# A retention layer with a low-rank mixer and MLP: paired batches, chunk-wise attention and an interleaved order of work

## Chip, cores, metric

One core of one Trainium2 chip. The metric is the device time of one execution in microseconds (us); lower is better. "Before" is the tuned kernel given, "after" the changed one. Matmuls write their results to PSUM; VectorE and ScalarE read them from there (an "evacuation").

## The reference

Batch 8, 8 heads, 576 tokens, head size 64, model width 512, MLP width 2048, mixer rank 32. Inputs and output are float32; both kernels calculate in bf16 with float32 accumulation.

```
scores = (q @ k.T) / sqrt(64);  ret = scores * gamma_h ** (i - j) for i >= j, else 0
x      = concat_heads(ret @ v)                      # 576 x 512 per batch
u      = x + (V.T @ U.T @ x)                        # mixer over tokens, rank 32
out    = u + relu(u @ w_ch1) @ w_ch2
```

Retention is computed in chunks of 128 tokens. gamma^i goes into q and gamma^-j into v. Within a chunk the scores are masked; across chunks a running state of k.T v is carried along. 576 = 4 x 128 + 64, so the last chunk is half full.

## The kernel before

Attention works on one pair of heads at a time, over all five chunks. `# ...` marks cuts.

```python
def attention_hp(hp, q_all, k_all, v_all, x_t):
    # ... transposes of q and k for 5 chunks, q scaled, k copied
    po = ps_out.tile([P, 8, P], FP32, tag="ps_out", name="po")
    for c in range(NC - 1):                       # running state, one matmul at a time
        nc.tensor.matmul(po[:, 5 + (c % 2), :], k2d, v2d, start=True, stop=True)
        # ... VectorE adds it to the state before, head by head (64 x 64)
    for c in range(NC - 1):                       # scores: 64 rows = one head
        for hl in range(2):
            pb = hl * 64
            nc.tensor.matmul(sc_h[hl][:, c, :], kT[pb:pb + 64, ...], qT[pb:pb + 64, ...], ...)
    # ... masks; then the scores of the last chunk, one matmul per head
    for c in range(NC):                           # ret @ v, 128 rows, 64 columns
        # ...
    for c in range(1, NC):                        # q @ state: 64 rows, 64 columns
        for hl in range(2):
            nc.tensor.matmul(po[:, slot, 0:64], qT[pb:pb + 64, ...], S_list[c - 1][pb:pb + 64, :], ...)
    # ... VectorE adds this to x

def mlp_tail(b, u_t, uT_t):
    for f in range(NF):                           # first layer: 2 x 288 columns
        for half in range(2):
            # 4 matmuls into ps_y1, then relu
    for tcn in range(NC):                         # second layer: 5 chunks, the last with 64 tokens
        for f in range(NF):
            nc.tensor.matmul(ps_y2[0:L, :], y1_t[:, f, tcn * P:tcn * P + L], w2_sb[:, f, :], ...)
        # ... add u, store
```

GpSimd issues all loads (they cast to bf16) and also scales v. A scheduler decides how attention of batch b+1 is mixed into the MLP of batch b.

## Time and profile before

| | before |
|---|---|
| median time | 432.16 us (13 runs, 431.71 to 432.77) |
| span of the profiled run | 430.0 us |
| first MLP matmul | 60.16 us |
| distance from batch to batch | 47.39 us |
| busy: TensorE / VectorE / ScalarE / GpSimd | 91 / 51 / 40 / 39 % |

TensorE is full from 60 us on. A full TensorE isn't yet one at its peak: its busy time is built from modelled ends, so what counts is the distance from one matmul's start to the next. The prediction shows the lines of this profile.

### The profile page before, as it was taken

To read this page: it belongs to the slowest core of one execution; us is meant where nothing else is said; L and a number is where in the kernel's file an instruction comes from. 1 tells how busy PE (TensorE), PEld (TensorE's weight loads), DVE (VectorE), ACT (ScalarE), POOL (GpSimd) and SP (SyncE) were. 2 spreads that over 40 slices of the span, in tenths; PEclk is the share of its full clock that TensorE was granted. 3 is DMA by queue.
4 is the path that set the end of the run, shared out by engine and by line. 5 is a ranking of instruction groups with operands and counts; after the bars stand their busy time and mean duration, and the time that the engine had idled before them with its cause. 6 is when DMAs were issued, how large, how long until landed. Compare 5 with 4: busy or idle time off the path is not lost.

```text
span 430.0 us, 8035 instructions
## 1 busy us (share of the span) xinstructions
PE 391.8 (91%) x3248; PEld 232.1 (54%) x3248; DVE 220.9 (51%) x662; ACT 171.9 (40%) x379; POOL 169.3 (39%) x220
## 2 busy tenths in 40 slices
PE   1256489999999999999999999999999999999996
PEld 0034256754675457644665467645765467546742
DVE  0166458751775448652875268643875277541011
ACT  2152136630564226630664136531663046423800
POOL 9999669999976700691048500000000000000000
PEclk9999999999999999999999999999999999999999
DMA  9999899999949910891079810011000100011011
GB/s 72 93 64 109 159 202 152 60 145 107 169 29 89 110 61 2 58 135 73 14 49 80 113 38 2 2 49 63 2 1 26 65 22 2 2 50 61 2 49 62
DMA packets 121333, 28.38 MB, mean 66 GB/s; under 512 B 114096, under 2 KB 116176, under 8 KB 121296
## 3 DMA queue, kind: packets, MB, share of 16 engines
q0 software_dynamic: 116048, 18.43, 57.8%
q1 hardware_dynamic: 5248, 9.44, 6.2%
q8 instruction: 25, 0.41, 0.4%
q14 instruction: 12, 0.10, 0.1%
HBM read 36.85 MB, written 9.44 MB: 108 GB/s over the span
## 4 chain that ended last, share of the span: by engine, by line
PE 87%; POOL 4%; DVE 4%; ACT 3%; issue 1%; DVEq 0%; ACTq 0%; POOLq 0%
PE ps_y L356 33%; PE ps_y L341 30%; PE po L185 3%; PE po L256 3%; PE ps_h L312 3%; PE blk_sc L219 3%; PE ps_at L301 2%; PE psq L164 2%; PE psk L174 2%; PE ps_ut L325 2%; PE po L271 2%; PE blk_sct L238 2%; ACT x_t L264 1%; POOL q_all L141 1%; POOL k_all L141 1%
## 5 line engine op out<-in xcount | busy, mean ns | idle before, releaser
L341 PE MATMUL ps_y<-uT_t,w_sb 128*128 128x288 bf16 x1024 | 155.3, 287 | 0.0
L356 PE MATMUL ps_y<-w_sb,y_t 128*128 128x512 bf16 (+1 forms) x640 | 149.6, 379 | 0.0
L347 ACT ACTIVATE y_t<-ps_y 128x288 bf16<-128x288 f32 x226 | 93.1, 412 | 62.7 <-PE ps_y L341 54.2
L341 PEld LDWEIGHTS <-w_sb 128*128 128x128 bf16 x1024 | 88.6, 98 | 27.8 <-issue 1.4
L356 PEld LDWEIGHTS <-y_t 128*128 128x128 bf16 (+1 forms) x640 | 61.5, 100 | 65.3 <-issue 3.4
L363 DVE TENSOR_TENSOR o_sb<-ps_y,u_t 128x512 f32<-128x512 f32 (+1 forms) x40 | 27.6, 690 | 99.5 <-PE ps_y L356 99.5
L177 ACT COPY kT<-psk 128x640 bf16<-128x640 bf16 x32 | 22.2, 693 | 95.7 <-PE psk L174 95.7
L200 DVE TENSOR_TENSOR S_cur<-po,S_cur 64x64 bf16<-64x64 f32 x192 | 42.3, 220 | 20.0 <-PE po L185 15.4
L227 DVE TENSOR_TENSOR ret_m<-blk_sc,maskbin 128x512 bf16<-128x512 f32 x64 | 42.5, 687 | 12.7 <-PE blk_sc L219 8.3
L150 POOL TENSOR_TENSOR v_all<-v_all,vscale 128x512 bf16<-128x512 bf16 x40 | 41.4, 1054 | 4.4 <-DMA v_all<-in_v_dram 3.9
L318 DVE TENSOR_TENSOR u_t<-ps_h,x_t 128x512 bf16<-128x512 f32 x40 | 27.6, 690 | 27.3 <-PE ps_h L312 27.3
L185 PE MATMUL po<-v_all,k_all 128*128 128x128 bf16 x128 | 29.2, 228 | 9.7 <-POOL v_all L150 4.7
L330 ACT COPY uT_t<-ps_ut 128x512 bf16<-128x512 bf16 x40 | 23.4, 586 | 33.8 <-PE ps_ut L325 33.8
L141 POOL DMA_DIRECT2D q_all<-in_q_dram x40 | 34.2, 875 | 0.0
L141 POOL DMA_DIRECT2D v_all<-in_v_dram x40 | 34.0, 912 | 0.0
L141 POOL DMA_DIRECT2D k_all<-in_k_dram x40 | 33.7, 874 | 0.0
L280 DVE TENSOR_TENSOR x_t<-po,x_t 128x192 bf16<-128x192 f32 x64 | 22.5, 351 | 7.8 <-PE po L271 5.5
L195 DVE CAST S_cur<-po 64x64 bf16<-64x64 f32 x64 | 14.1, 220 | 24.0 <-PE po L185 23.5
L264 ACT CAST x_t<-po 128x512 bf16<-128x512 f32 x31 | 18.2, 586 | 17.7 <-PE po L256 16.9
L164 PE MATMUL psq<-ident,q_all 128*128 128x128 bf16 x160 | 16.4, 230 | 8.8 <-DMA q_all<-in_q_dram 8.7
L138 POOL MEMSET q_all<- 64x512 bf16 x8 | 4.2, 520 | 50.2 <-PE psq L164 50.0
L185 PEld LDWEIGHTS <-k_all 128*128 128x128 bf16 x128 | 12.7, 100 | 18.4 <-issue 4.4
(50 smaller groups left out, 313.5 us busy)
## 6 DMA issues: line engine op xcount, KB each, us to landing
out_dram<-o_sb SPq DMA_DIRECT2D x32, 256.0 KB, 2.0
q_all<-in_q_dram POOLq DMA_DIRECT2D x32, 128.0 KB, 4.3
k_all<-in_k_dram POOLq DMA_DIRECT2D x32, 128.0 KB, 4.4
v_all<-in_v_dram POOLq DMA_DIRECT2D x32, 128.0 KB, 4.6
w_sb<-in_moe_w_ch_dram POOLq DMA_DIRECT2D x4, 512.0 KB, 7.5
w_sb<-in_moe_w_ch_dram POOLq DMA_DIRECT2D x16, 128.0 KB, 5.3
out_dram<-o_sb SPq DMA_DIRECT2D x8, 128.0 KB, 2.2
q_all<-in_q_dram POOLq DMA_DIRECT2D x8, 64.0 KB, 4.8
```

The lines of the kernel that those rows point to most:

```text
L141: nc.gpsimd.dma_start(out=t_sb[0:L, c, :, :], in_=t_dram[b, :, c * P:c * P + L, :].rearrange("h s d -> s h d"),)
L150: nc.gpsimd.tensor_tensor(out=v_all[:, c, :, :], in0=v_all[:, c, :, :], in1=vs_b[:, c, :, :], op=ALU.mult,)
L164: nc.tensor.transpose(psq[:, c, :], q2d, ident)
L185: nc.tensor.matmul(po[:, 5 + (c % 2), :], k2d, v2d, start=True, stop=True,)
L200: nc.vector.tensor_tensor(out=S_cur[pb:pb + 64, :], in0=po[pb:pb + 64, 5 + (c % 2), pb:pb + 64], in1=S_list[c - 1][pb:pb + 64, :], op=ALU.add,
L227: nc.vector.tensor_tensor(out=rt_h[hl][:, :, :], in0=sc_h[hl][:, :, :], in1=maskbin[:, None, :].to_broadcast([P, 4, P]), op=ALU.mult,)
L318: nc.vector.tensor_tensor(out=u_t[:, c, :], in0=ps_h, in1=x_t[:, c, :], op=ALU.add)
L330: nc.any.tensor_copy(out=uT_t[:, :, c * P:(c + 1) * P], in_=ps_ut[:, 0:NCC, :])
L341: nc.tensor.matmul(ps_y1[:, 0:HTOK], w1_sb[:, cc, f * P:(f + 1) * P], uT_t[:, cc, t0:t0 + HTOK], start=(cc == 0), stop=(cc == NCC - 1),)
L347: nc.any.tensor_scalar(out=y1_t[:, f, t0:t0 + HTOK], in0=ps_y1[:, 0:HTOK], scalar1=0.0, scalar2=None, op0=ALU.max,)
L356: nc.tensor.matmul(ps_y2[0:L, :], y1_t[:, f, tcn * P:tcn * P + L], w2_sb[:, f, :], start=(f == 0), stop=(f == NF - 1),)
L363: nc.vector.tensor_tensor(out=o_sb[0:L, :], in0=ps_y2[0:L, :], in1=u_t[0:L, tcn, :], op=ALU.add,)
```

## The change

Its intent is to do less on TensorE and to keep it fed evenly:

1. two batches share their half-full chunks, so that an even batch has 4 and an odd batch 5 full chunks in the MLP (mean 4.5 instead of 5);
2. attention goes chunk by chunk over all heads; the running state stays in PSUM and is read by one VectorE operation per chunk for all heads (masked to its diagonal blocks, which makes q @ state a matmul on all 128 rows); gamma^i is applied at the output;
3. loads go chunk by chunk (k, q, v), and v of the first two batches is scaled on VectorE;
4. an explicit order spreads attention and mixer items evenly through the MLP;
5. small PSUM pools have one buffer each; relu is on ScalarE only.

The diff, cut to its core (`...` marks cuts; most lines of the kernel changed):

```diff
+def interleave(main, fill):
+    ...
+        if j >= len(fill) or (i < len(main) and dm / tm <= df / tf):   # next MLP item
+        ...                                                              # else next attention item
-    def attention_hp(hp, q_all, k_all, v_all, x_t): ...
+    def load_chunk(b, c):
+        for j, dram in ((1, k), (0, q), (2, v)):
+            nc.gpsimd.dma_start(out=t[rows, j, :, :], in_=dram[b, :, t0:t0 + L, :]...)
+        (nc.vector if b < 2 else nc.gpsimd).tensor_tensor(out=t[rows, 2, :, :], ...)   # scale v
+        def ST(c):                                  # state of all heads, accumulated in PSUM
+            for hp in range(NHP):
+                nc.tensor.matmul(pss[:, hp, :], k..., v...,
+                    start=(c == 0 and hp == 0), stop=True, skip_group_check=True)
+            nc.vector.tensor_tensor(out=s_sb, in0=pss, in1=bdm..., op=ALU.mult)
+        def SC(c):                                  # eight score matmuls together
+            for hp in range(NHP):
+                for hl in range(2):
+                    pb = hl * HALF
+                    nc.tensor.matmul(psc[:, hl, hp, 0:n], qkT[pb:pb + HALF, NHP + hp, :],
+                                     qkT[pb:pb + HALF, hp, cols], start=True, stop=True)
+        def RV(c):                                  # ret @ v, then q @ state on 128 rows
+            ...
+                    nc.tensor.matmul(po[:, hp * P:(hp + 1) * P], qkT[:, hp, :], s_sb[:, hp, :],
+                                     start=False, stop=True, skip_group_check=True)
-        for f in range(NF):
-            for half in range(2): ...               # 128 matmuls of 288 columns a batch
+        nch = 4 if par == 0 else 5
+        segs = [(0, 512)] if par == 0 else [(0, 320), (320, 320)]
+    early_consts(); zero_halves(); load_batch(0); late_consts()
+    load_batch(1); load_w1(); load_w2()
+    interleave([], front_items(0))
+    for b in range(B): ...
+            interleave(mlp_items(b, us[b], pairs[b // 2]), fill)
```

## The prediction

> **What bounds the kernel now.** I read the page first, for the busy shares and the 40 slices.
>
> ```profile
> span 430.0 us, 8035 instructions
> PE 391.8 (91%) x3248; PEld 232.1 (54%) x3248; DVE 220.9 (51%) x662; ACT 171.9 (40%) x379; POOL 169.3 (39%) x220
> ...
> PE   1256489999999999999999999999999999999996
> ...
> POOL 9999669999976700691048500000000000000000
> ```
>
> TensorE is the only engine that is full, and it is full from the sixth slice (10.75 us each) on. Two questions remain: how much of the full stretch is real matmul work, and what fills the first 60 us, in which TensorE is mostly idle. For the first I read the chain that ended last, in order of time.
>
> ```profile
> 89.14 0.86 PE ps_at L301 x4
> ...
> 136.53 0.86 PE ps_at L301 x4
> ...
> 183.92 0.86 PE ps_at L301 x4
> ...
> 392.94 15.79 PE ps_y L341 x128
> 408.72 17.40 PE ps_y L356 x80
> ```
>
> Every batch passes the same point 47.39 us after the one before. The last batch's MLP runs alone at the end and shows the bare rates: 15.79/128 = 123 ns for a first-layer matmul (288 columns), 17.40/80 = 217.5 ns for a second-layer one (512 columns). So 33.19 us of a period is bare MLP; the other 47.39 - 33.19 = 14.20 us is the next batch's attention and mixer. Last matmul at 426.12 us, so counting back 8 x 33.19 + 7 x 14.20 = 364.9 puts the start of this regime at 61.2 us. The timeline of the start confirms it and shows what comes before:
>
> ```profile
> 6.16 0.29 PE L164 MATMUL psq<-ident,q_all 128*128 128x128 bf16 x1 [6.16 <-DMA q_all<-in_q_dram]
> ...
> 16.10 4.09 POOL L150 TENSOR_TENSOR v_all<-v_all,vscale 128x512 bf16<-128x512 bf16 x4
> ...
> 25.32 4.27 POOL L141 DMA_DIRECT2D q_all<-in_q_dram  x5
> ...
> 43.44 0.62 POOL L125 DMA_DIRECT2D w_sb<-in_moe_w_ch_dram  x1
> ...
> 60.16 1.17 PE L341 MATMUL ps_y<-uT_t,w_sb 128*128 128x288 bf16 x4
> ```
>
> Batch 0's data have all landed by about 16 to 18 us, but its attention (four head pairs one after the other through one PSUM tile) and mixer end only at 60 us. GpSimd meanwhile alternates between issuing loads, scaling v and making constants, so the first weights are asked for at 43.44 us.
>
> **What the Trainium skill says.** "TensorE: Matmul & The Clock Gate", section "Wait — 56ns, not 53.3ns?", gives start-to-start N/2.4 + about 2.5 ns when warm: 55.6 ns for 128 columns, 215.7 for 512. The trace agrees: five transposes start at 213.72 and the next five at 214.00, 56 ns each, and the bare 512-column rate is 217.5. "Perfetto Trace Analysis", section "Tensor Engine Instruction (MATMUL, LD_WEIGHTS)", says that the profile's end time for TensorE is an estimate; so I use distances between starts, not the 287 and 379 ns of the groups (the trace agrees: 379 ns each cannot fit a 217 ns pitch). "DMA: Bandwidth & Descriptors", section "SWDGE vs HWDGE vs iDMA", says that a DMA that casts must be issued from GpSimd; all loads here cast float32 to bf16 and all are GpSimd's, so their issue order is one queue. "PSUM — Partial Sum Buffer", section "The four PSUM rules", says that a partial sum may be read in the middle of an accumulation group; the change's running state relies on it, and this trace doesn't show it.
>
> **The change, part by part.**
> *Padding.* Tokens are paired over two batches: an even batch runs 4 full chunks in the MLP, an odd one 5, sharing the 64-row remainder. First layer: the columns stay the same (64 matmuls x 512, or 128 x 320, against 128 x 288). Second layer: 80 matmuls of 512 columns become 64 or 80, mean 72, since a 64-row chunk costs as much as a full one. Saved: 8 x 217.5 ns = 1.74 us a batch. MLP per batch: 15.79 + 15.66 = 31.45 us.
> *Small matmuls.* Before, per batch: 40 transposes of q and k, 16 state, 40 score, 40 ret-times-v, 32 state-times-q, 20 transposes of u: 188, plus 10 mixer matmuls of 512 columns (10 x 217.5 = 2.18 us). The rest of the 14.20, 12.02 us, makes 64 ns each, switches between kinds included. After: the 32 become 16 of 128 rows by 128 columns, the 20 become 18 in the mean: 170. At the same 64 ns that is 10.88 + 2.18 = 13.06 us, saving 1.14.
> *Period.* 31.45 + 13.06 = 44.5 us against 47.4: about 2.9 saved.
> *Interleaving.* Items of attention and mixer are spread evenly through the MLP. The order of the built kernel shows groups of 4 or 8 small matmuls with 4 to 8 MLP matmuls (0.55 to 1.7 us) between them. All small PSUM pools have one buffer, so each item's evacuation must fit there. Mostly it does. Where an even batch's MLP begins, only four state matmuls (0.22 us) cover the last 512-column ScalarE copy (586 ns plus signalling, say 0.85): some 0.6 us lost, three times. Adding similar bits at masks of 1024 elements, I allow 4 us in all.
> *ScalarE.* Per-element cost from its 640- and 512-element copies: (693 - 586)/128 = 0.836 ns. So 40 copies of 1024 at 1014 ns = 40.6; rectifying 64 x 586 + 128 x 439 = 93.7; 36 + 8 other copies at 586 = 25.8. Sum 160 us, as before. *VectorE*: 32 masks of 1024 at about 1225 ns (slope (687 - 351)/320 = 1.05) and 8 of 512, 44.7; state 32 x 687 = 22.0; scaling by q at the output, 40 x 690 = 27.6; u 27.6; outputs 36 x 692 = 24.9; v scaling of two batches about 7. Sum 154 against 221. Neither is near the bound, so VectorE's 67 us of relief are worth nothing by themselves.
> *Start.* Loads go out chunk by chunk (k, q, v), with no scaling on GpSimd for the first two batches. Five issues take 4.27 us, so a batch takes 12.8 us. Beginning at 1.9, batch 0 is issued by 14.7, five small constants (about 3.2 us) by 18, batch 1 by 30.8. Landing comes 4.0 to 4.6 us after issue, so batch 0's last chunk is there at 18.5. Its chain is then held back by VectorE's order: scalings of batch 1's chunks (landing at 23.3, 25.8, 28.6, 31.4) stand ahead of batch 0's last x and u. That puts the end of batch 0's mixer at about 34. The first four weight pieces are issued from 30.8 to 33.1 and take 5.3 us: 38. The later of the two counts: the MLP starts at 38 instead of 60 to 61. The rest of the weights come at some 200 GB/s (the best slice of before shows 202), 2 MB a matrix in 10 us, faster than they are used.
> *Sum.* 38 + 8 x 31.45 + 7 x 13.06 + tail 3.9 (430.0 - 426.1) = 384.9; with 4 for waits 388.9; times are 1.8 above the span (431.83 against 430.0): 390.7, say 390. About 22 of the gain are the start, about 20 the steady part.
>
> **The rivals.**
> First, *the start gains little*. If the loads of two batches and the weights hinder one another and the weights land at 50, the time is 402; if batch 0 is again a chain until 60, 413. For it: the DMA row stands at 9 throughout the start. Against: landings follow issues by a steady 4 us there, so the queue isn't backing up, and chunks let the chain begin at 8 us.
> Second, *single buffers turn into TensorE waits*. Some 34 items a batch; 0.2 us exposed at each would be 34 x 0.2 x 7 = 48 us and eat the gain: 438. Against: between an item and the next user of its PSUM stand at least two other items; only 1014 and 1225 ns evacuations behind a busy queue could exceed that.
> Third, *ScalarE becomes the bound in the first layer*. There it has 16 x 586 + 5 x 1014 = 14.4 us (even) or 32 x 439 + 5070 = 19.1 (odd) in about 25 us. It fits, but strict order could hold a rectification behind a 1014 ns copy: up to 2 us a batch, 405.
> Fourth, *GpSimd falls behind*: 12.8 us of issues, five scalings of 1.05 and waits for five landings of about 4 make 38 us a batch under a 44.5 us period; it also works a batch ahead. I expect nothing from it.
>
> **Range and chances.** 390 us; the start could be off by 8 either way, the period by 1 us (7 us): 379 to 402. Missing 423 needs the second rival in force or two others together. Faster 0.95, within 2% 0.04, slower 0.01.
>
> **What would show it.** First MLP matmul near 38 us, after the weights and not after uT; a mean period of two batches near 89 us; 768 first-layer matmuls and 576 second-layer ones at unchanged pitch; idle TensorE after the start under 8 us; ScalarE near 160, VectorE near 154 us. I am wrong if the MLP starts after 50, if TensorE waits for ScalarE or VectorE add to over 20 us past the start, or if the granted clock falls below the 1.00 of before.

## The result

| | before | after | predicted for after |
|---|---|---|---|
| median time | 432.16 us (13 runs) | 369.09 us (8 runs, 368.17 to 369.77) | 390 (379 to 402) |
| span of the profiled run | 430.0 | 368.1 | 388.9 |
| first MLP matmul | 60.16 | 36.39 | 38 |
| two batches | 94.78 | 84.32 | 89 |
| busy TensorE / VectorE / ScalarE | 391.8 / 220.9 / 171.9 | 346.0 / 157.3 / 155.8 | - / 154 / 160 |

The ratio is 0.8538 (95% interval 0.8527 to 0.8549). A ratio is the mean time of one kernel's fast runs over that of the other's of the same rounds, so it isn't quite the ratio of the medians quoted. The output is correct. The direction was right, but the time fell below the range: the kernel is 21 us faster than predicted.

The page of the changed kernel first. The columns of the middle rows are 40 slices of 9.2 us, in tenths.

```profile
span 368.1 us, 6528 instructions
...
PE 346.0 (94%) x2784; PEld 198.9 (54%) x2784; DVE 157.3 (43%) x223; ACT 155.8 (42%) x279; POOL 151.1 (41%) x189
...
PE   1756999999999999999999999999999999999995
...
PEclk9995899999999999999999999999999999999999
...
L399 PE MATMUL ps_y<-w_sb,y 128*128 128x512 bf16 x576 | 143.2, 379 | 0.0
```

TensorE is full from the fifth slice on, with 576 second-layer matmuls as predicted. The granted clock dips in slices 4 and 5: TensorE had idled, and began its MLP at half speed. Now the start of the MLP and the period, from the chain of what ended last:

```profile
38.06 2.32 PE ps_y L388 x6
...
77.59 1.09 PE ps_y L388 x8
...
161.91 1.09 PE ps_y L388 x8
...
246.23 1.09 PE ps_y L388 x8
...
329.94 17.00 PE ps_y L388 x124
346.94 17.28 PE ps_y L399 x80
```

The same point returns every 84.32 us, that is two batches. At the end an odd batch's MLP runs alone: 17.00/124 = 137 ns for 320 columns, 17.28/80 = 216 ns for 512. The bare pitches are those predicted. So bare MLP is 128 x 0.1371 + 17.28 = 34.83 us for an odd batch and 128 x 0.216 = 27.65 for an even one, 31.24 in the mean; attention and mixer take (84.32 - 62.48)/2 = 10.92 us a batch, where 13.06 were predicted.

**Where 62 us went.** For each pair of successive matmuls in the two traces I took the distance between starts and subtracted columns/2.4 + 2.5 ns, the pitch that full-row matmuls of one kind keep in both traces. The rest is excess. (Both traces hold all their matmuls: 3248 and 2784. Most later runs lack some 37 records, so their sums aren't used.)

| from the first MLP matmul to the last start | before | after | saved |
|---|---|---|---|
| time ahead of it | 60.2 us | 36.4 us | 23.8 |
| pitch of all matmuls | 338.5 | 321.3 | 17.2 |
| excess, in all | 27.1 | 6.1 | 21.0 |
| - change between 128 and 64 rows | 194 x 106 ns = 20.5 | 70 x 94 ns = 6.6 | 13.9 |
| - change of line on the same rows (mostly waits, see below) | 460 x 25 ns = 11.5 | 405 x 10 ns = 4.2 | 7.3 |
| - next to each other on 64 rows | 407 x -18 ns = -7.3 | 245 x -27 ns = -6.6 | -0.7 |
| - same line | 2.4 | 1.9 | 0.5 |

Start and pitch are near what was predicted. The excess isn't: the prediction had carried most of it over. Half-row matmuls (scores; before also q @ state) start closer together than the pitch (27 ns less in the changed kernel, where two heads on different rows alternate), but going into and out of them costs about 95 ns each way. The timeline shows it. Columns are start, length, engine, line, operation; the last number is how many. Before, in a steady stretch:

```profile
212.41 0.65 PE L341 MATMUL ps_y<-uT_t,w_sb 128*128 128x288 bf16 x4
213.00 0.23 PE L238 MATMUL blk_sct<-qT,kT 64*128 64x128 bf16 x1
213.16 0.54 PE L341 MATMUL ps_y<-uT_t,w_sb 128*128 128x288 bf16 x3
213.54 0.22 PE L185 MATMUL po<-v_all,k_all 128*128 128x128 bf16 x1
213.59 0.29 PE L341 MATMUL ps_y<-uT_t,w_sb 128*128 128x288 bf16 x1
```

Four first-layer matmuls take 0.59 us before a single half-row score, 0.10 more than 4 x 122.5 ns; the score itself occupies 0.16 instead of 0.06. The three after it, followed by a full-row matmul, take 0.38, only 0.01 more than 3 x 122.5. After:

```profile
214.00 1.03 PE L388 MATMUL ps_y<-uT,w_sb 128*128 128x512 bf16 x4
214.86 0.39 PE L223 MATMUL pss<-qkv 128*128 128x128 bf16 x4
215.08 1.03 PE L388 MATMUL ps_y<-uT,w_sb 128*128 128x512 bf16 x4
216.04 0.40 PE L244 MATMUL psc<-qkT 64*128 64x128 bf16 x8
216.37 1.04 PE L388 MATMUL ps_y<-uT,w_sb 128*128 128x512 bf16 x4
```

Four MLP matmuls take 0.86 us ahead of the full-row state and 0.96 ahead of the half-row scores. But now eight scores stand together, in 0.33 us with the change back, and q @ state no longer uses half rows.

**Changes and waits told apart.** The trace also has the semaphore updates that a matmul or its weight load waits for (a semaphore is the counter by which one engine tells another that it is done). In the kernel before, some matmuls start 41 to 46 ns after the last of these updates; they were waiting. The sums by this test:

| us of excess | before | after |
|---|---|---|
| row changes without a wait | 166 x 96 ns = 15.9 | 70 x 94 ns = 6.6 |
| row changes that end a wait | 28 x 164 ns = 4.6 | 0 |
| same rows, ending a wait | 119 x 89 ns = 10.6 | 14 x 286 ns = 4.0 |
| same rows, other line, no wait | 334 x 0.6 ns = 0.2 | 392 x 1.3 ns = 0.5 |

So a change of line costs nothing by itself; the 25 ns above are a mean of waits and of zeros. An example of a wait, to set beside the 0.01 us ahead of the state matmul at 213.54:

```profile
214.38 0.90 PE L341 MATMUL ps_y<-uT_t,w_sb 128*128 128x288 bf16 x6
215.23 0.39 PE L256 MATMUL po<-v_all,ret_m 128*128 128x64 bf16 x8
```

Six MLP matmuls take 0.85 us instead of 0.74 although both sides use all rows; the update that the second line waited for came at 215.18. Counting 96 ns of each change as the change's own, row changes cost 18.6 us before and 6.6 after, and waits 12.5 and 4.0: of the 21.0 us saved, 12.0 are row changes and 8.5 are waits. About 12 of the 15 us in the two wait rows of before end on an update by VectorE, most of them its state additions and the u additions. One more change costs the same: 15 changes between 128 and 64 active columns (the last, half-full chunk of the second layer) took 94 ns each before, 1.4 us; the changed kernel has none.

### The profile page after: what moved, and what is told of

It is laid out like the page before. It is cut to its first block, busy times and chain, and to the rows that moved or that the text cites. A ratio compares the mean times of both kernels' runs of the same rounds, so it can differ in the third digit from the quotient of the medians.

```text
span 368.1 us, 6528 instructions
## 1 busy us (share of the span) xinstructions
PE 346.0 (94%) x2784; PEld 198.9 (54%) x2784; DVE 157.3 (43%) x223; ACT 155.8 (42%) x279; POOL 151.1 (41%) x189
## 4 chain that ended last, share of the span: by engine, by line
PE 87%; POOL 7%; DMA 3%; ACT 2%; issue 0%; DVE 0%; POOLq 0%
PE ps_y L399 34%; PE ps_y L388 34%; POOL qkv L179 5%; PE pst L205 4%; PE psc L244 3%; PE po L268 2%; PE ph L333 2%; PE psa L320 2%; PE pu L349 2%; PE po L275 2%; DMA qkv<-in_v_dram 2%; PE pss L223 1%; DMA w_sb<-in_moe_w_ch_dram 1%; ACT qkTh L214 1%; ACT uT L352 1%; POOL qkvh L179 1%
## 5 line engine op out<-in xcount | busy, mean ns | idle before, releaser
L388 PE MATMUL ps_y<-uT,w_sb 128*128 128x320 bf16 (+1 forms) x768 | 143.4, 328 | 1.6 <-ACT uT L352 1.4
L399 PE MATMUL ps_y<-w_sb,y 128*128 128x512 bf16 x576 | 143.2, 379 | 0.0
L392 ACT ACTIVATE y<-ps_y 128x320 bf16<-128x320 f32 (+1 forms) x192 | 92.1, 490 | 39.5 <-PE ps_y L388 32.4
L399 PEld LDWEIGHTS <-y 128*128 128x128 bf16 x576 | 53.6, 98 | 55.4
L183 POOL TENSOR_TENSOR qkv<-qkv,vscale 128x512 bf16<-128x512 bf16 x24 | 24.9, 1039 | 63.4 <-DMA qkv<-in_v_dram 63.3
L255 DVE TENSOR_TENSOR ret<-psc,tri 128x1024 bf16<-128x1024 f32 x32 | 39.1, 1222 | 13.5 <-PE psc L244 13.5
L214 ACT ACTIVATE qkT<-pst 128x1024 bf16<-128x1024 bf16 x32 | 32.8, 1024 | 10.6 <-PE pst L205 10.0
L179 POOL DMA_DIRECT2D qkv<-in_k_dram x32 | 29.7, 930 | 7.8 <-PE po L268 5.0
L179 POOL DMA_DIRECT2D qkv<-in_v_dram x32 | 29.2, 913 | 0.8 <-DMA w_sb<-in_moe_w_ch_dram 0.8
L179 POOL DMA_DIRECT2D qkv<-in_q_dram x32 | 28.9, 903 | 0.6 <-DMA w_sb<-in_moe_w_ch_dram 0.4
L342 DVE TENSOR_TENSOR ut<-ph,xt 128x512 bf16<-128x512 f32 x32 | 22.0, 690 | 10.7 <-PE ph L333 10.5
```

The lines of the kernel that those rows point to most:

```text
L179: nc.gpsimd.dma_start(out=t[rows, j, :, :], in_=dram[b, :, t0:t0 + L, :].rearrange("h s d -> s h d"),)
L183: (nc.vector if b < 2 else nc.gpsimd).tensor_tensor(out=t[rows, 2, :, :], in0=t[rows, 2, :, :], in1=vscale[rows, c, :, None].to_broadcast( ...
L214: nc.scalar.activation(out=qkT, in_=pst, func=AF.Copy)
L255: nc.vector.tensor_tensor(out=rv[:, :, :, cols], in0=psc[:, :, :, 0:n], in1=tri[:, None, None, cols].to_broadcast([P, 2, NHP, n]), op=ALU. ...
L388: nc.tensor.matmul(ps[:, 0:n], w1_sb[:, cc, f * P:(f + 1) * P], uT[:, cc, t0:t0 + n], start=(cc == 0), stop=(cc == NCC - 1),)
L392: nc.scalar.activation(out=st["y1"][:, f, t0:t0 + n], in_=ps[:, 0:n], func=AF.Relu)
```

## The experiments

Fifteen kernels, with the changed kernel's 0.8538 to compare ratios with. Differences below some 0.3% between different calls mean nothing.

### Splitting the scores

Each chunk's scores in two groups of four:

```diff
-                add(SC, s - 1, 450)
+                add(lambda c: SC(c, 0), s - 1, 225)      # head pairs 0, 1
+                add(lambda c: SC(c, 1), s - 1, 225)      # head pairs 2, 3, then the mask
```

> Changed kernel with each chunk's eight score matmuls split into two groups of four, MLP matmuls between them. Theory (half-row switches): every change between matmuls on 128 rows and on 64 rows costs TensorE about 95 ns (trace of the changed kernel: 70 such changes, mean excess 94 ns). The built order has 110 changes instead of 70 and 20 fewer side-by-side pairs of half-row matmuls (27 ns each): +40 x 94 + 20 x 27 = +4.3 us, so about 373.4 against 369.1. Rival (any interruption of the MLP stream costs the same, about 25 ns or less each): about +0.3 us, no visible change.

Measured: 373.04 us (6 runs, 371.48 to 375.36), ratio 0.8637 (0.8610 to 0.8664), 4.0 us over the changed kernel, as the theory says. In its steady stretch:

```profile
167.74 0.71 PE L393 MATMUL ps_y<-uT,w_sb 128*128 128x320 bf16 x4
168.38 0.29 PE L246 MATMUL psc<-qkT 64*128 64x128 bf16 x4
168.60 0.72 PE L393 MATMUL ps_y<-uT,w_sb 128*128 128x320 bf16 x4
169.25 0.28 PE L246 MATMUL psc<-qkT 64*128 64x128 bf16 x4
```

Each of the two groups is paid for with 0.10 us in the MLP matmuls before it (0.64 and 0.65 us instead of 4 x 0.136).

### Control: splitting the transposes

```diff
-                add(T, s, 460)
+                add(lambda c: T(c, 0), s, 230)           # q
+                add(lambda c: T(c, 1), s, 230)           # k, then the copy
```

> Control: the eight transposes of a chunk split into two groups of four in the same way, all on 128 rows. Row changes stay at 70, changes between lines on the same rows rise from 405 to 456. Theory (half-row switches): 51 x 10 ns = +0.5 us, not visible. Rival (any interruption costs the same): as much as splitting the scores, 4 us if that costs 4.

Measured: 368.42 us, ratio 0.8527 (0.8514 to 0.8539). The same cut in full-row work costs nothing. So it is not interruption as such, but the change of rows.

### Scores on all rows

```diff
-                        qkT[pb:pb + HALF, NHP + hp, :],
-                        qkT[pb:pb + HALF, hp, cols],
+                        qkT[:, NHP + hp, :],
+                        qkT[:, hp, cols],
```

> Wrong result on purpose: the score matmuls of the changed kernel read all 128 rows, so there is no change of rows at all. Theory: 70 changes x 94 ns = -6.6 us, the lost side-by-side running of half-row pairs +6.6 us (245 x 27 ns), plus about 10 ns at each former change: net 0 to +1 us, 369 to 370; in the trace the 94 ns excess before and after scores is gone and each score matmul takes 56 instead of about 27 ns. Rival (excess is from waiting for the evacuated inputs of the scores): the excess stays and the time rises by 6 to 7 us.

Measured: 369.07 us, ratio 0.8534 (0.8517 to 0.8550); wrong result. The order of instructions is the same:

```profile
214.84 1.03 PE L388 MATMUL ps_y<-uT,w_sb 128*128 128x512 bf16 x4
215.70 0.61 PE L244 MATMUL psc<-qkT 128*128 128x128 bf16 x8
216.15 1.03 PE L388 MATMUL ps_y<-uT,w_sb 128*128 128x512 bf16 x4
217.01 0.61 PE L205 MATMUL pst<-ident,qkv 128*128 128x128 bf16 x8
```

The 0.10 us ahead of the scores is gone (0.86 again) and the eight scores take 0.45 instead of 0.33 us: the two effects cancel, as expected. With the order of instructions unchanged, the excess follows the rows: the 70 places that cost 92 to 96 ns each in the changed kernel cost -1 to 1 ns here.

### The kernel before on all rows

```diff
-                    kT[pb:pb + 64, c * P:(c + 1) * P],   # scores, twice; q @ state likewise
-                    qT[pb:pb + 64, c * P:(c + 1) * P],
+                    kT[:, c * P:(c + 1) * P],
+                    qT[:, c * P:(c + 1) * P],
```

> Wrong result on purpose: the kernel before with its scores and its state-times-q matmuls on all 128 rows. Its trace has 194 row changes with 106 ns excess (20.5 us) and 7.3 us saved by half-row pairs. Theory: -20.5 + 7.3 + 194 x 25 ns (ordinary change of line) = -8.4 us, so about 424 against 432. Rival (the excess comes from semaphores, not from rows): +7 us, 439.

Measured: 428.31 us, ratio 0.9913 (0.9900 to 0.9925); wrong result. The sign is the theory's, the size under half of it: -3.7 us instead of -8.4. In its trace (17 matmul records are missing) 675 changes of line have a mean excess of 34 ns, not the 25 that I had counted with. Entering the former half-row groups still costs: 129 ns for q @ state after the first layer (155 before), 46 for the single scores (100 before). Leaving the single scores (98 ns before) does become free. What stays on entry is waiting, by the test above: with the row changes gone TensorE comes to its operands earlier, and they aren't ready. Waits rise from 12.5 us to some 19 (an estimate: the excess of 26.2 us less the 3.7 of the missing records, the column changes and the rest). The sum, -18.6 + 7.3 + 6.5 = -4.8 us, is near the -3.7 measured. The two don't add at one entry: the seven entries into q @ state at 158 to 160 ns in the kernel before take 160 on equal rows too, so the later of wait and row change counts.

### Putting the padding back

```diff
+        if par == 0:
+            for f0 in range(0, NF, 4):
+                items.append((853, lambda f0=f0: Y2(3, f0, False)))   # chunk 3 again, not stored
```

> Puts the padding back alone: even batches run their fourth chunk of the second layer a second time without storing it, so that the second layer has 640 matmuls again instead of 576. Theory (TensorE is the bound, at the bare pitch): 64 x 215.8 ns = +13.8 us, 383. Rival (matmuls hidden behind another bound): less than 7.

Measured: 382.69 us, ratio 0.8857 (0.8841 to 0.8873): +13.6 us for +13.8 expected. The padding's share of the gain is its matmuls at the bare pitch.

### The start: scaling v on GpSimd again

```diff
-        (nc.vector if b < 2 else nc.gpsimd).tensor_tensor(
+        nc.gpsimd.tensor_tensor(
```

> Undoes one part of the start: v of the first two batches is scaled on GpSimd again, as before, instead of on VectorE. Theory: GpSimd's queue holds all load issues; ten scalings of 1.04 us and the waits for ten v landings (some 1 to 2 us each, as the scaling stands one or two issues behind its load) delay the first weights by 12 to 20 us; a few us of batch 1's attention then run before the MLP instead of in it, so the time rises by about 12: 381 (376 to 386), first MLP matmul at 48 to 55 us instead of 36. Rival (batch 0's own chain of attention and mixer sets the start, not the weights): under 3 us more.

Measured: 379.83 us, ratio 0.8799 (0.8786 to 0.8812): +10.7. The weights are the wait:

```profile
44.65 0.90 PE L205 MATMUL pst<-ident,qkv 128*128 128x128 bf16 x7 [0.20 <-ACT qkT L214]
47.76 9.61 PE L388 MATMUL ps_y<-uT,w_sb 128*128 128x512 bf16 x35 [2.21 <-DMA w_sb<-in_moe_w_ch_dram]
```

### The start: loading tensor by tensor

```diff
-        for j, dram in ((1, k), (0, q), (2, v)):        # inside one chunk
+        for j, dram in ((1, k), (0, q), (2, v)):
+            for c in range(NC): ...                     # all chunks of one tensor
```

> Undoes another part of the start: all chunks of k, then of q, then of v are loaded, instead of k, q, v chunk by chunk. Theory (the first weights, issued after the same 30 loads, set the start at 36 us; batch 0's chain ends about 1 us before them): 0 to +3 us, 369 to 372. Rival (arrival chunk by chunk is what gained the start): +5 us or more, as v of chunk 0 lands at 13 instead of 8 us.

Measured: 374.16 us, ratio 0.8665 (0.8653 to 0.8677): +5.1, which is the rival's number. The wait ahead of the first MLP matmul is now for batch 0's own last copy:

```profile
41.90 1.02 PE L394 MATMUL ps_y<-uT,w_sb 128*128 128x512 bf16 x4 [0.36 <-ACT uT L358]
```

So my theory that only the weights set the start falls. Arrival by chunk and free issue are both needed.

### The start: v scaled on VectorE in the kernel before

```diff
-            nc.gpsimd.tensor_tensor(
+            (nc.vector if b < 2 else nc.gpsimd).tensor_tensor(
                 out=v_all[:, c, :, :], ...
```

> Kernel before with one part of the change's start alone: v of the first two batches scaled on VectorE, so that GpSimd issues the loads of both batches and the weights without a stop (weights from about 34 instead of 43 us). Theory (before, batch 0's chain of four head pairs and the mixer sets the start, and the weights were not waited for): under 3 us gained, 429 to 432. Rival (earlier weights are the gain of the start): 415 to 422.

Measured: 433.75 us, ratio 1.0029 (1.0012 to 1.0046): no gain. Its first weights are asked for at 33.58 us instead of 43.44, and the MLP still begins at 61.3:

```profile
33.58 2.29 POOL L125 DMA_DIRECT2D w_sb<-in_moe_w_ch_dram  x4
```

Batch 0's chain through four head pairs is the limit there. That chunk-wise attention is what lets earlier loads count follows from this and `a_tmajor` together; no run tested it alone.

### Trying to start earlier still

Four kernels, from the changed one: `a_start` loads half of w1 before batch 1 and puts the scaling of batch 1's v after batch 0's items; `a_warm` adds dummy matmuls in the mixer of batch 0; `a_b1pool` is `a_start` with batch 1's v scaled on GpSimd; `a_b1pool_warm` has both.

```diff
-    load_batch(1)
-    load_w1()
+    load_w1([0, 1]); load_batch(1); load_w1([2, 3])     # a_start; v of batch 1 scaled later
+            for _ in range(2):                           # a_warm, after each mixer step of batch 0
+                nc.tensor.matmul(st["w"], ident, rhs, start=True, stop=True)
+    for c in range(NC): scale_chunk(1, c, qkv[1][c])     # a_b1pool: on GpSimd, before load_w1([2, 3])
```

> Attempt at a better start: the first two of four weight blocks are loaded before batch 1, and the scalings of batch 1's v come after batch 0's items in program order, so that VectorE doesn't wait for batch 1 in the middle of batch 0's chain. Theory: the chain of batch 0 then ends at 30 to 32 us, the weights land at 27: first MLP matmul at about 31 instead of 36.4, batch 1's data just in time: 364 (362 to 367). Rival (batch 1's later landing stops the interleaved attention): no gain, 369 or more.

> Changed kernel with two dummy matmuls of 512 columns after each mixer step of batch 0, on the data of that step, to keep TensorE active before the MLP. Theory: the trace shows the first MLP matmuls at 393 ns instead of 215 until 40 us, some 2 to 4 us lost in all with the slow mixer steps before them; 366 to 369. Rival (the dummies stand in the way of batch 0's chain): 369 to 372.

> Second attempt at the start: half of the first-layer weights before batch 1, and batch 1's v scaled on GpSimd after its loads, so that nothing of batch 1 stands in VectorE's queue before batch 0's u. Theory: the gap of 3.2 us that the first attempt showed before u is gone, first MLP matmul at about 34.5 instead of 36.4; the second half of the first-layer weights comes later (about 47) and may cost 1 to 2 us: 367 to 370.

> Both together: first MLP matmul at about 33.5 and at full pitch: 364 to 368.

Measured: 370.26, 369.93, 371.98 and 372.69 us (ratios 0.8574, 0.8561, 0.8604, 0.8614). None gains. `a_start` left one of batch 1's scalings ahead of batch 0's u in VectorE's queue, and VectorE waited for that load:

```profile
30.91 0.69 DVE L174 TENSOR_TENSOR qkvh<-qkvh,vscale 64x512 bf16<-64x512 bf16 x1 [3.46 <-DMA qkvh<-in_v_dram]
31.63 1.29 DVE L348 TENSOR_TENSOR ut<-ph,xt 128x512 bf16<-128x512 f32 x2
```

`a_warm` removed the slow clock (0.999 granted instead of 0.981; the slow matmuls stand 427 ns apart in the changed kernel's trace, not 393), but the MLP then caught up with the weights, which land piece by piece:

```profile
35.99 0.39 PE L399 MATMUL ps_y<-uT,w_sb 128*128 128x512 bf16 x1 [0.57 <-DMA w_sb<-in_moe_w_ch_dram]
36.63 0.39 PE L399 MATMUL ps_y<-uT,w_sb 128*128 128x512 bf16 x1 [0.25 <-DMA w_sb<-in_moe_w_ch_dram]
37.36 0.39 PE L399 MATMUL ps_y<-uT,w_sb 128*128 128x512 bf16 x1 [0.34 <-DMA w_sb<-in_moe_w_ch_dram]
```

`a_b1pool` began at 36.05, still after a slow chain, and waited for the second half of the weights at 49.41 us (1.07). Chain, clock and weights lie close together at 36 us; moving one shows the next.

### Giving VectorE its work back

Twice: two idle operations after each output, tied to nothing (`a_dve_fill`); then one after each x, u and output of batches 1 to 7 (after every output also of batch 0), tied to that tile or its input (`a_dve_fill2`).

```diff
+                nc.vector.tensor_tensor(out=filler, in0=filler, in1=filler, op=ALU.max)   # a_dve_fill, twice
+                nc.vector.tensor_tensor(out=filler, in0=o_sb, in1=o_sb, op=ALU.max)       # a_dve_fill2; likewise for x, u
```

> Gives VectorE back about the work it lost (72 idle operations of 768 float32 elements, an estimate of 0.8 to 0.9 us each, some 60 us, two after each output). Theory (TensorE alone bounds the steady part, VectorE's relief of 64 us is worth nothing by itself): 369 to 371, VectorE busy about 220 us. Rival (the gain came from VectorE's relief): 380 or more.

> The filler experiment again, with each idle VectorE operation tied to the tile just written (one after each x, u and output of batches 1 to 7: 106 operations of 512 elements, an estimate of 0.69 us each, 70 us), so that they are spread evenly and none runs before its batch; the first attempt's ran together at the start. VectorE then has about 227 us, as the kernel before (221). Theory (relief of VectorE is worth little, as its evacuations have a MLP group's time of slack): 369 to 373. Rival (VectorE's relief is what removed the waits of the fill): 380 or more.

Measured: 382.81 us (three fast runs, ratio 0.8856; a fourth, slow, took 387.24) and 371.95 us (ratio 0.8605, 0.8589 to 0.8622). The first can't tell the theories apart: the scheduler ran its filler in one heap, as VectorE's row of the page shows:

```profile
DVE  7898799999999995553344534543343533550021
```

There TensorE waited for masks (9.2 us). The second spread evenly to 228.0 us of VectorE work, as much as before the change, and cost 2.9 us. So VectorE's relief is worth little by itself in the changed kernel, as the prediction said, though not nothing. It doesn't speak for the kernel before, whose waits ended mostly on VectorE (some 12 us, see above): there the order in which its results came counted, which a filler doesn't test.

### An attention item first

```diff
-        if j >= len(fill) or (i < len(main) and dm / tm <= df / tf):
+        if j >= len(fill) or (i < len(main) and dm / tm < df / tf):
```

> Changed kernel with the interleaving starting with an attention item instead of an MLP item (strict comparison in one place), so that transposes stand between the last copy of uT and the first MLP matmul of an even batch. Theory: the three waits of 0.63 us there shrink: -1 to -2 us, 367 to 368. Rival (the scheduler's order leaves them): no change.

Measured: 368.91 us, ratio 0.8529 (0.8516 to 0.8543): not told apart from the change's 0.8538. The wait only moved, from the MLP matmul of the changed kernel to a transpose, which now needs the single transpose buffer that the copy of uT still holds:

```profile
PE pst L205 <- ACT uT L352: 1.4, 3, 0.5
```

In the changed kernel the line was this, with the same total, count and longest:

```profile
PE ps_y L388 <- ACT uT L352: 1.4, 3, 0.5
```

No version found here beats the changed kernel beyond the noise.

## Why the prediction was wrong

Point by point, in the order of its sum:

| term | predicted | measured | difference |
|---|---|---|---|
| start | 38 | 36.4 | -1.6 |
| 8 bare MLPs | 8 x 31.45 | 8 x 31.24 | -1.7 |
| 7 attentions and mixers | 7 x 13.06 | 7 x 10.92 | -15.0 |
| waits on top | 4 | inside the line above | -4.0 |
| tail | 3.9 | 3.9 | 0 |
| first MLP on a half-speed clock | not foreseen | about +1.4 | +1.4 |
| span | 388.9 | 368.1 | -20.8 |

(The +1.4 is the first even batch's 41.20 us, 36.39 to 77.59, against 39.77, from 122.14 to 161.91, of a later one. The rounded rows add to -20.9.)

**Right.** TensorE's bound, its bare pitches, 768 and 576 MLP matmuls, 1.74 us a batch for the padding (the padding run: 13.6 of 13.8 us), ScalarE and VectorE within 5 us, the start within 2. The three waits of about 0.6 us at the beginning of an even batch's MLP are there. The rivals didn't come true: single buffers hid their evacuations, and TensorE's waits after the start add to 4.0 us. The running state, read after every chunk, gave correct outputs.

**The step that failed**: "At the same 64 ns that is 10.88 + 2.18 = 13.06 us". The 64 ns were the kernel before's 12.02 us over its 188 small matmuls, "switches between kinds included", and I scaled them with the number of matmuls. But their pitch was only about 8.6 us of it (116 of 128 columns at 55.8 ns, 72 of 64 columns at 29.2). The rest was excess, which goes not with the number of matmuls but with changes between full and half rows (194 before, 70 after, while the small matmuls fell only from 188 to 170 a batch) and with waits for operands (12.5 us before, 4.0 after). The waits of before were in the 64 ns, so with 4 us on top the sum counted waits twice. The measured small work is 10.92 - 2.16 = 8.76 us, 51.5 ns each. The experiments bear this out in the changed kernel: 40 more row changes cost 4.0 us, the same cut in full-row work nothing, and with equal rows the excess at those places vanishes. In the kernel before equal rows make the exits free and uncover more waits on entry, as its semaphores show. That the new order of work is what shortened the waits is argued; no run tested it alone.

I could have counted. The changed kernel's order of instructions was there to read and holds 70 row changes; the trace of before holds 194; and the Trainium skill names the cause: "TensorEngine Tiling (Array Packing)", section "Key Properties", says that changing the tiling mode drains the TensorE. The traces agree in the cost, at 94 ns a change after the change; that it is a drain they don't show. 124 changes x 97 ns are 12.0 us and the shorter waits 8.5; less the tenth of the old excess that the prediction had itself taken off (3.0 us), that is some 17.5 of the 19.0 us (15.0 and 4.0) by which those two lines of the table differ.

**Wrong mechanism of the start, right number.** I had the weights as the later of two limits and four us between them. In the trace batch 0's chain ended, with the last copy of uT, at 35.93 us, just 0.41 us before the first weights were there (36.34), and loading by tensor (+5.1 us) showed that the chain counts. The granted clock fell, which I had named as a sign of being wrong; it cost about 1.4 us and isn't the cause.

## What to carry to other kernels

Split the time of small matmuls into their pitch, the changes of rows or columns, and waits, before scaling it to a new kernel: the first goes with matmuls, the second with the number of groups whose rows or columns differ from their neighbours', the third with when operands are ready. Look at single cases and not only at means: 25 ns a change of line was a mean of zeros and of waits. Keep half-row matmuls together, and rewrite those that can use all rows without more columns. Here the start had gained from a shorter chain of the first tile and earlier loads together; moving one further alone gained nothing.

## What the Trainium skill lacked or had wrong

- "TensorEngine Tiling (Array Packing)", "Key Properties", says that a mode switch drains TensorE, without a cost: about 94 ns each way in the changed kernel (70 changes of rows), 4.0 us for 40 more of them, and 94 ns for each of 15 changes of columns in the kernel before. Two heads next to each other on half rows win back 27 ns a matmul, so that for groups of eight score matmuls half and full rows took the same time (369.07 against 369.09 us).
- "TensorE: Matmul & The Clock Gate", "Back-to-back issue gap", gives 81 ns for 128 columns and 131 for 512 as the sustained pitch of weight load and matmul pairs. Here such pairs ran at 56 ns (transposes) and 216 ns (80 second-layer matmuls in 17.28 us), the numbers that the section calls isolated.
- No page says that such a change and a wait for operands don't add: entries into q @ state took 158 to 160 ns in the kernel before, and 160 with equal rows.
